# Scores of the first batch from keys in place, and a new order with an engine for each step

## The chip, the cores and the metric

The kernel runs on one core of a Trainium2 chip. Its engines work side by side: TensorE (PE) multiplies matrices, VectorE (DVE) and ScalarE (ACT) work element by element, GpSimd (POOL) does so too but can't read the matrix results in PSUM, and SyncE (SP) issues most of the loads and stores. The metric is the device time of one execution in microseconds; lower is better.

## The reference

Three layers follow one another. The first is attention over 2 batches, 8 heads, 768 positions and 64 columns a head: each query sees the keys less than 16 positions away and, beside them, 24 block summaries (for the keys the maximum of each block of 32, for the values the mean).

```
k_sum = k.reshape(B, H, nb, block, D).max(axis=3)
v_sum = v.reshape(B, H, nb, block, D).mean(axis=3)
scores_l = scale * (q @ k.T), masked to |i - j| < 16
scores_s = scale * (q @ k_sum.T) + log(32)
a = softmax(concat(scores_l, scores_s)); attn = a @ concat(v, v_sum)
h = x @ w_in;  g = max(h, 0) + alpha * min(h, 0);  x = g @ w_out
p = domain_probs / (sum + 1e-9)
out = sum over 4 experts e of p[:, e] * (max(x @ w1[e], 0) @ w2[e])
```

The second layer is a PReLU layer of 512 x 2048 x 512 on 1536 tokens, the third four experts of 512 x 1024 x 512. Everything is float32.

## The kernel before

**Precision.** A float32 factor of the two later layers is split into a high part and the rest, and a product is done as three passes of a faster format. So each activation and weight needs a high part (a copy) and a low part (source minus high part).

**Attention.** A half tile is one batch, 128 queries and four of the eight heads, as two blocks of 64 queries for two pairs of heads: 24 half tiles, numbered 0 to 23, the first twelve in batch 0. Its steps are a chain over the engines. `a_scores` (L199) multiplies the queries with a window tile `kw` of 120 columns, 96 keys around the query block and the 24 block maxima, four products. `a_max` (L207) adds the mask and takes the maximum on VectorE, `a_exp` (L220) is on ScalarE, `a_guard` and `a_recip` (L229, L233) are small VectorE steps, `a_norm` (L236) scales by the reciprocal with four ScalarE instructions, `a_transpose` is on TensorE, `a_copy` (L247) on ScalarE, `a_pv` (L252) multiplies with the values. `a_xh` (ScalarE) and `a_xl` (VectorE) split the result into `xh` and `xl`.

The window tiles come from a copy of the keys that is laid out window by window in memory (`load_kw`, L184, 192 KB a half tile). The block maxima come from the plain keys: `k_load` (L155) brings 384 KB for two heads into a tile `kv`, `k_max` (L158) reduces it on VectorE into `ksum`, and `k_copy` (L161) copies the maxima into both window tiles of a pair of heads. Values go through `v_load`, `v_sum`, `v_rows` and `v_mean` in the same way.

**Weights.** The weights of the PReLU layer arrive as 64-bit numbers and are turned into float32 by integer steps, 32 pieces of 128 x 512: `w_load`, `w_mask` (L294), `w_exp` (ScalarE, L299), `w_mant`, `w_frac` (L311), `w_top`, `w_sign`, `w_value` (L325), `w_high` (ScalarE, L329), `w_low` (L335). All others are on VectorE. `w_mask`, `w_mant` and `w_top` have one tensor as input, the other VectorE steps two.

**PReLU layer, first quarter.** The first four of 16 column groups are done for six blocks of 256 tokens, as soon as a block's half tiles are through. `l1_product` makes 12 passes, four such products a block; `l1_minus`, `l1_prelu`, `l1_high`, `l1_low` follow, then four products `l2a_product` of 12 passes each and their sum into `acc` by `l2a_sum`.

**Order.** All this is written out in `ORDER`, a table of two letters and numbers per step: `sa4` is the scores of half tile 4, `la00` the first product of block 0, `wb5` the mask step of piece 5. Each engine does its steps strictly in the order of the table, and SyncE issues its loads so as well (`wa` weights, `ka`, `va` keys and values for the summaries, `fa` windows, `fb` queries, `fc` value windows). A load waits for its buffer: 3 of queries, 2 of `kv`, 3 of raw weights, 2 of values. The rest of the PReLU layer (512-wide products, from `pa` on) and the experts follow behind the table and are not touched. GpSimd has work only from the experts' first weights on (L366, L373 to L376).

Of the kernel before, what the change touches and what calls it, by code (L numbers as in the profile page):

```python
# [8 lines left out]
F32 = mybir.dt.float32  # L9
# [82 lines left out]
def kernel(  # L92
# [30 lines left out]
    ebias = cst.tile([P, 1], F32, name="ebias")  # L123
    prob_sb = cst.tile([P, NT, NE], F32, name="prob_sb")
# [6 lines left out]

    ident = att1.tile([P, P], F32, name="ident")
    mask = att1.tile([P, 3, NK], F32, name="mask")
    ksum = att1.tile([P, HP, 1, NB], F32, name="ksum")

    kwb = [[att1.tile([P, NK // NB, 2, 2, NB], F32, name=f"kw{hh}{i}") for i in range(2)] for hh in range(2)]
    vs = att1.tile([P, HP, NK], F32, name="vs")
# [8 lines left out]
    def half_tile(i):  # L146
        b, r = divmod(i, 2 * NAC)
        return b, r // 2, r % 2
# [638 lines left out]
```

## Time and profile before

| | |
|---|---|
| three runs | 854.04, 854.30 and 855.51 us, median 854.3 us |
| profiled execution | 854.7 us, of it span 852.9 us |
| TensorE | busy 824.0 us, 97 % of the span |
| VectorE, ScalarE, GpSimd | busy 64 %, 47 % and 39 % |
| loads and stores | 76.61 MB, mean 90 GB/s |

A share over the whole span says little here: the first stretch, with the attention, has other limits than the rest. Times of the views count from the first instruction. A "wait" names what released an engine that stood idle.

### The profile page before, as it was taken

What the parts mean: (1) busy time and instruction counts of PE and PEld (TensorE: products, weight loads), DVE (VectorE), ACT (ScalarE), POOL (GpSimd) and SP (SyncE); (2) the same over time, 40 slices, a digit from 0 to 9 for tenths busy, and PEclk for the clock granted to TensorE, in tenths of its full rate; (3) what the DMA queues carried; (4) which work ended last, traced back from release to release, by engine and by line L of the source; (5) the groups of instructions that cost most, each with busy time, mean ns of one, the idle gap of its engine ahead of it and who ended that gap; (6) DMA issues with size and microseconds to landing.
All of it is one profiled execution on the core that took longest, in us unless ns stands there. A gap on an engine that the chain in (4) does not pass through costs nothing.

```text
span 852.9 us, 12751 instructions
## 1 busy us (share of the span) xinstructions
PE 824.0 (97%) x4622; PEld 734.4 (86%) x4622; DVE 548.9 (64%) x1144; ACT 402.2 (47%) x987; POOL 328.4 (39%) x326
## 2 busy tenths in 40 slices
PE   2799999999999999999999999999999999999998
PEld 2689999888888888989989988888899899898997
DVE  7898566999995446455555567856655555555555
ACT  4999995534443323343343434434534434334340
POOL 0000000000014200376575676775676666756730
PEclk9899999999999999999999999999999999999999
DMA  8998530223221000112213113122322131131201
GB/s 286 290 288 265 155 115 27 98 99 100 86 82 55 26 1 0 50 51 79 71 50 98 51 50 99 50 66 82 125 75 75 50 95 54 50 99 50 75 2 74
DMA packets 39695, 76.61 MB, mean 90 GB/s; under 512 B 3792, under 2 KB 15568, under 8 KB 39632
## 3 DMA queue, kind: packets, MB, share of 16 engines
q1 hardware_dynamic: 39056, 75.51, 27.8%
q8 instruction: 36, 0.59, 0.3%
q10 hardware_dynamic: 576, 0.28, 0.1%
q14 instruction: 27, 0.22, 0.1%
HBM read 72.63 MB, written 3.15 MB: 89 GB/s over the span
## 4 chain that ended last, share of the span: by engine, by line
PE 89%; DVE 6%; DMA 3%; ACT 2%; SPq 0%; issue 0%; ACTq 0%
PE l L413 59%; PE cb L522 15%; PE cd L522 7%; PE ca L522 4%; DMA raw<-in_wa 2%; PE s L205 2%; DVE acc L501 1%; DMA q<-in_qh 1%; PE xps L263 1%; DVE acc L608 1%; PE pt L245 1%; DVE ksum L159 1%; DVE sm L215 0%; DVE xel L483 0%; ACT sm L224 0%
## 5 line engine op out<-in xcount | busy, mean ns | idle before, releaser
L366 POOL TENSOR_TENSOR w0l<-ra,w0h 128x512 fp32r<-128x512 f32 (+1 forms) x64 | 71.1, 1111 | 351.1 <-DVE acc L472 248.3
L608 DVE SCALAR_TENSOR_TENSOR acc<-l,prob_sb,acc 128x512 f32<-128x512 f32 x179 | 133.8, 750 | 74.6 <-PE l L413 74.6
L413 PE MATMUL l<-w1h,gh 128*128 128x512 f32 (+1 forms) x386 | 149.8, 388 | 1.1 <-DVE acc L608 1.1
L413 PE MATMUL l<-w1h,gl 128*128 128x512 f32 (+1 forms) x386 | 150.4, 390 | 0.0
L413 PE MATMUL l<-w1l,gh 128*128 128x512 f32 (+1 forms) x386 | 150.3, 389 | 0.0
L366 POOL TENSOR_TENSOR w0l<-s,w0h 128x512 fp32r<-128x512 f32 x64 | 85.7, 1360 | 5.6 <-ACT w0h L365 5.6
L366 POOL TENSOR_TENSOR w1l<-rb,w1h 128x512 fp32r<-128x512 f32 x64 | 82.0, 1302 | 11.9 <-ACT w1h L365 11.9
L413 PEld LDWEIGHTS l<-w1h,gh 128*128 128x128 f32 x386 | 72.5, 188 | 15.8 <-DVE acc L608 1.6
L413 PEld LDWEIGHTS l<-w1h,gl 128*128 128x128 f32 x386 | 72.4, 188 | 15.0
L413 PE MATMUL l<-xh,w0h 128*128 128x512 f32 (+1 forms) x240 | 84.7, 353 | 0.2 <-ACT ptb L250 0.2
L413 PEld LDWEIGHTS l<-w1l,gh 128*128 128x128 f32 x386 | 72.5, 188 | 14.3
L413 PE MATMUL l<-xl,w0h 128*128 128x512 f32 (+1 forms) x240 | 83.2, 347 | 0.0
L413 PE MATMUL l<-gh,w1h 128*128 128x512 f32 (+1 forms) x240 | 83.1, 350 | 0.0
L413 PE MATMUL l<-xh,w0l 128*128 128x512 f32 (+1 forms) x240 | 83.1, 346 | 0.0
L413 PE MATMUL l<-gh,w1l 128*128 128x512 f32 (+1 forms) x240 | 83.0, 347 | 0.0
L532 ACT ACTIVATE p<-cb 128x384 f32<-128x384 f32 x32 | 15.7, 492 | 140.0 <-PE cb L522 140.0
L413 PE MATMUL l<-gl,w1h 128*128 128x512 f32 (+1 forms) x240 | 80.9, 347 | 0.0
L373 POOL TENSOR_TENSOR s<-ra 128x256 f32<-128x256 f32 x32 | 23.6, 738 | 123.8 <-DMA ra<-in_wb 120.0
L522 PE MATMUL cb<-xeh,w0h 128*128 128x384 f32 x192 | 64.4, 335 | 0.2
L522 PE MATMUL cb<-xeh,w0l 128*128 128x384 f32 x192 | 64.2, 334 | 0.0
L522 PE MATMUL cb<-xel,w0h 128*128 128x384 f32 x192 | 64.2, 334 | 0.0
L539 DVE SCALAR_TENSOR_TENSOR gl<-cb,gh 128x384 fp32r<-128x384 f32 x32 | 17.8, 557 | 55.3 <-ACT gh L538 55.3
(103 smaller groups left out, 1857.2 us busy)
## 6 DMA issues: line engine op xcount, KB each, us to landing
raw<-in_wa SPq DMA_DIRECT2D x32, 512.0 KB, 3.4
ra<-in_wb SPq DMA_DIRECT2D x64, 256.0 KB, 3.1
rb<-in_wb SPq DMA_DIRECT2D x32, 512.0 KB, 3.6
q<-in_qh SPq DMA_DIRECT2D x24, 256.0 KB, 4.9
kw<-in_kw SPq DMA_DIRECT2D x24, 192.0 KB, 5.1
vcat<-in_vw SPq DMA_DIRECT2D x12, 384.0 KB, 5.7
kv<-in_kt SPq DMA_DIRECT2D x8, 384.0 KB, 5.6
kv<-in_vt SPq DMA_DIRECT2D x8, 384.0 KB, 4.7
```

Of the source, the lines that this page charges most:

```text
L159: nc.vector.tensor_reduce(ksum[:, hp, 0], st.pop(("k", b, hp)), axis=AX.X, op=ALU.max)
L205: nc.tensor.matmul(sp[:, u], q[:, u // 2, u % 2], kw[:, :, u // 2, u % 2], start=True, stop=True)
L245: nc.tensor.transpose(pt[0:NK, u], pp[:, u], ident)
L263: nc.tensor.matmul(xps[j * D:(j + 1) * D, u // 2, qb * QB:(qb + 1) * QB], vc[0:NK, qb, h * D:(h + 1) * D], ptb[0:NK, u, j * D:(j + 1) * D] ...
L366: nc.gpsimd.tensor_tensor(lo, src, hi.bitcast(F32), op=ALU.subtract)
L373: nc.gpsimd.tensor_tensor(s12[:, 0], r[:, 0], r[:, 3], op=ALU.add)
L413: ins = nc.tensor.matmul(ps, a, c, start=(i == 0), stop=(i == n - 1))
L501: nc.vector.tensor_tensor(y, p, q, op=ALU.subtract)
L522: nc.tensor.matmul(ps, l, r, start=(first and i == 0), stop=(i == len(terms) - 1), skip_group_check=True)
L532: nc.scalar.activation(v[name], ps, AF.Copy)
L539: nc.vector.scalar_tensor_tensor(gl, src, 0.0, gh.bitcast(F32), op0=ALU.max, op1=ALU.subtract)
L608: nc.vector.scalar_tensor_tensor(acc2[:, t], ps, pe, acc2[:, t], op0=ALU.mult, op1=ALU.add)
```

## The change

Four edits.

The keys of batch 0 are loaded into `kt`, the half of the accumulator `acc1` that belongs to batch 1 and isn't written until the fourth token block's sums. The block maxima are reduced from there, and the scores of batch 0 read keys and maxima in place: one product of 96 columns (two, of 80 and 16, for a block at the start or end of the sequence) and one of 24. `load_kw` and `k_copy` are then used for batch 1 only.

Steps may carry an engine: a trailing `g` in the table puts a normalization (now one instruction of 128 x 480), a `w_value` or a `w_low` on GpSimd, a trailing `v` puts a copy, a ReLU or a normalization on VectorE in place of ScalarE. In the new table 16 normalizations, 13 `w_value` and 11 `w_low` stand on GpSimd, and 39 steps on VectorE that were ScalarE's (9 sums, 8 high parts, 7 `xh`, 6 `l1_minus`, 3 `a_copy`, 3 normalizations, 2 `w_high`, 1 `w_exp`), the first of them behind the second token block's four products.

The table is a new one throughout.

An Exp of a small constant stands at ScalarE's start.

```
 ORDER = (
-    "wa0 ka00 wb0 ka01 wd0 wc0 we0 wa5 fb4 wf0 wg0 kb00 wh0 wa2 fa4 wb5 fa0 fb0 wi0 wc5 wj0 ka02 kb01 "
+    "wa0 wa1 wb0 wd0 we0 ka03 wc0 wd1 wf0 wb1 ka02 wg0 wh0g fb1 ka01 kb03 kb02 sa1 we1 ka00 kb01 wc1 "
...
+    early = cst.tile([P, 1], F32, name="early")
...
-    ksum = att1.tile([P, HP, 1, NB], F32, name="ksum")
+    ksum = att1.tile([P, B, HP, 1, NB], F32, name="ksum")
...
+    def copy(dst, src, on="a"):
+        if on == "v":
+            nc.vector.tensor_copy(dst, src)
+        else:
+            nc.scalar.activation(dst, src, AF.Copy)
...
+    kt = acc1[:, 1]
+
     def k_load(b, hp):
-        st["k", b, hp] = load_kv(kt_in, b, hp)
+        if b == 0:
+            nc.sync.dma_start(out=kt[:, hp], in_=kt_in[b, hp])
+            st["k", b, hp] = kt[:, hp].rearrange("p (n k) -> p n k", k=BLK)
+        else:
+            st["k", b, hp] = load_kv(kt_in, b, hp)
...
     def a_scores(i):
         b, ac, hh = half_tile(i)
-        q, kw = st.pop(("q", i)), st.pop(("kw", i))
+        q = st.pop(("q", i))
+        st["s", i] = sp = ps_s.tile([P, 4, NK], F32, tag="s", name="s")
+        if b == 0:
+            for u in range(4):
+                hp, c0 = 2 * hh + u // 2, (2 * ac + u % 2) * QB - WIN
+                runs = [(0, KW, c0)]
+                if c0 < 0:
+                    runs = [(WIN, KW, 0), (0, WIN, 0)]
+                elif c0 + KW > S:
+                    runs = [(0, KW - WIN, c0), (KW - WIN, KW, S - WIN)]
+                for a, z, c in runs:
+                    nc.tensor.matmul(sp[:, u, a:z], q[:, u // 2, u % 2], kt[:, hp, c:c + z - a], start=True, stop=True)
+                nc.tensor.matmul(sp[:, u, KW:NK], q[:, u // 2, u % 2], ksum[:, b, hp, 0], start=True, stop=True)
+            return
+        kw = st.pop(("kw", i))
...
-    def a_norm(i):
+    def a_norm(i, on="a"):
         pp, r = st["p", i], st.pop(("r", i))
+        if on != "a":
+            eng = nc.vector if on == "v" else nc.gpsimd
+            eng.tensor_tensor(pp, pp, r[:, :, None].to_broadcast([P, 4, NK]), op=ALU.mult)
+            return
...
-    def w_value(p):
+    def w_value(p, on="v"):
         _, e, t = pw[p]
-        nc.vector.tensor_tensor(t, t, e, op=ALU.mult)
-
-    def w_high(p):
+        (nc.gpsimd if on == "g" else nc.vector).tensor_tensor(t, t, e, op=ALU.mult)
+
+    def w_high(p, on="a"):
...
-    def w_low(p):
+    def w_low(p, on="v"):
...
-        nc.vector.tensor_tensor(lo, pw.pop(p)[2], ws[k, i].bitcast(F32), op=ALU.subtract)
+        eng = nc.gpsimd if on == "g" else nc.vector
+        eng.tensor_tensor(lo, pw.pop(p)[2], ws[k, i].bitcast(F32), op=ALU.subtract)
...
     nc.gpsimd.memset(vs, 0.0)
+    nc.scalar.activation(early, ebias, AF.Exp)
...
-            a = x[2:]
-            ins = stage[x[:2]](*((int(a),) if x[0] in "fsntxw" else [int(c) for c in a]))
+            a, on = (x[2:-1], x[-1:]) if x[-1] in "vg" else (x[2:], "")
+            ins = stage[x[:2]](*((int(a),) if x[0] in "fsntxw" else [int(c) for c in a]), *on)
```

On TensorE, the program's first scores before (`s` the scores in PSUM, `kw` a window tile, `q` the queries, `pt` a transpose):

```order
L205 MATMUL s<-kw_96,q 128x120 x4
L205 MATMUL s<-kw_97,q 128x120 x4
L205 MATMUL s<-kw_98,q 128x120 x4
L205 MATMUL s<-kw_99,q 128x120 x4
L245 MATMUL pt<-ident,sm 120x128 x8
```

The same place in the change (`acc` holds the keys, `ksum` the maxima):

```order
L225 MATMUL s<-acc,q 128x80
L225 MATMUL s<-acc,q 128x16
L226 MATMUL s<-ksum,q 128x24
L225 MATMUL s<-acc,q 128x96
L226 MATMUL s<-ksum,q 128x24
```

A query block has two products, or three at an edge, where it had one; half tile 1 is now first, half tile 4 was.

On VectorE, ahead of the first scores before (`ksum` the reduction of keys, `t` and `e` a weight piece's numbers, `w0l` its low part):

```order
L327 TENSOR_TENSOR t<-t,e 128x512
L671 TENSOR_SCALAR prob_s<-prob_s 128x12
L296 TENSOR_SCALAR e<-raw 128x512
L672 RECIPROCAL prob_s<-prob_s 128x12
L673 TENSOR_TENSOR prob_sb<-prob_sb,prob_s 128x48
L338 TENSOR_TENSOR w0l<-t,w0h 128x512
L159 TENSOR_REDUCE ksum<-kv 128x24
L306 TENSOR_SCALAR t<-raw 128x512
L317 TENSOR_SCALAR e<-e 128x512
L296 TENSOR_SCALAR e<-raw 128x512
L163 COPY kw_96<-ksum 128x96
L163 COPY kw_97<-ksum 128x96
```

The same stretch in the change:

```order
L354 SCALAR_TENSOR_TENSOR e<-raw,e 128x512
L172 TENSOR_REDUCE ksum<-acc 128x24
L708 TENSOR_REDUCE prob_s<-prob_sb 128x12
L172 TENSOR_REDUCE ksum<-acc 128x24
L346 SCALAR_TENSOR_TENSOR t<-raw,t 128x512
L709 TENSOR_SCALAR prob_s<-prob_s 128x12
L172 TENSOR_REDUCE ksum<-acc 128x24
L350 TENSOR_SCALAR e<-e 128x512
```

The copies into window tiles are gone, the reductions stand closer together, and the value and low part of the first piece have left VectorE.

On GpSimd, its first tensor work before, which belongs to the experts' weights:

```order
L366 TENSOR_TENSOR w0l<-ra,w0h 128x256
L373 TENSOR_TENSOR s_3602<-ra 128x256
L374 TENSOR_TENSOR s_3602<-s_3602,ra 128x256
L375 TENSOR_TENSOR s_3603<-ra 128x256
L376 TENSOR_TENSOR s_3603<-ra,s_3602 128x256
```

GpSimd's first tensor work in the change (`sm` the probabilities, `r` their reciprocal sums):

```order
L360 TENSOR_TENSOR t<-t,e 128x512
L372 TENSOR_TENSOR w0l<-t,w0h 128x512
L360 TENSOR_TENSOR t<-t,e 128x512
L266 TENSOR_TENSOR sm<-sm,r 128x480 x3
L360 TENSOR_TENSOR t<-t,e 128x512
L266 TENSOR_TENSOR sm<-sm,r 128x480
L372 TENSOR_TENSOR w0l<-t,w0h 128x512
```

Forty such instructions now stand on GpSimd ahead of the experts' first.

## Rows read from the trace of the kernel before

**Rows 1.** Windows: stretch, its us, busy us (instructions) PE, PEld, DVE, ACT, POOL, clock, DMA

```profile
0.00:46.66 46.66, 24.32 (x177) 20.89 (x177) 38.16 (x146) 33.18 (x116) 0.74 (x6) 0.93 0.89 285
46.66:157.03 110.37, 108.51 (x1095) 103.48 (x1094) 81.26 (x300) 92.39 (x327) 0.00 (x0) 1.00 0.53 163
157.03:260.00 102.97, 102.97 (x457) 85.28 (x456) 98.19 (x186) 45.65 (x79) 4.83 (x5) 1.00 0.27 90
```

**Rows 2.** Timeline of TensorE: start, us, operation, [idle before, releaser]

```profile
13.87 3.77 PE L205 MATMUL s<-kw,q 128*128 128x120 f32 x16 [13.87 <-DVE kw L163]
...
45.77 1.12 PE L205 MATMUL s<-kw,q 128*128 128x120 f32 x8 [0.80 <-DMA kw<-in_kw]
46.66 0.36 PE L413 MATMUL l<-xh,w0h 128*128 128x256 f32 x1
...
157.03 0.40 PE L413 MATMUL l<-xh,w0h 128*128 128x512 f32 x1
```

**Rows 3.** Timeline of VectorE ahead of the first product

```profile
5.09 0.43 DVE L296 TENSOR_SCALAR e<-raw 128x512 uint32<-128x512 uint32 x1 [5.09 <-DMA raw<-in_wa]
...
7.65 0.43 DVE L317 TENSOR_SCALAR e<-e 128x512 uint32<-128x512 f32 x1 [1.07 <-ACT e L301]
...
34.99 1.31 DVE L182 TENSOR_SCALAR vcat<-vsps 24x512 f32<-24x512 f32 x2
...
45.55 0.41 DVE L280 TENSOR_TENSOR xl<-xps,xh 128x256 fp32r<-128x256 f32 x1
```

**Rows 4.** Windows: the first 50 us; the last two are DMA share and GB/s

```profile
0.00:50.00 50.00, 27.66 (x225) 24.02 (x226) 41.50 (x161) 36.43 (x128) 0.74 (x6) 0.93 0.90 285
```

**Rows 5.** Chain of waits, VectorE's pitch: start, us, engine, tile, line

```profile
9.84 0.60 DVE t L327
...
11.83 0.86 DVE ksum L159
12.69 0.33 DVE t L306
...
13.70 0.24 DVE kw L163 x2
...
16.28 0.20 DVE sm L215
```

**Rows 6.** The costliest groups: GpSimd's 512-wide low parts, busy us, mean ns

```profile
L366 POOL TENSOR_TENSOR w1l<-rb,w1h 128x512 fp32r<-128x512 f32 x64 | 82.0, 1302 | 11.9 <-ACT w1h L365 11.9
```

**Rows 7.** Timelines of GpSimd and VectorE, 249 to 260 us

```profile
249.61 1.11 POOL L366 TENSOR_TENSOR w0l<-ra,w0h 128x256 fp32r<-128x256 f32 x1 [248.35 <-DVE acc L472]
...
258.14 1.18 POOL L376 TENSOR_TENSOR s<-ra,s 128x256 f32<-128x256 f32 x1
...
250.12 0.88 DVE L317 TENSOR_SCALAR e<-e 128x512 uint32<-128x512 f32 x1
...
253.73 0.67 DVE L327 TENSOR_TENSOR t<-t,e 128x512 f32<-128x512 f32 x1
...
257.93 0.79 DVE L313 SCALAR_TENSOR_TENSOR t<-raw,t 128x512 f32<-128x512 uint32 x1
...
258.76 1.11 DVE L327 TENSOR_TENSOR t<-t,e 128x512 f32<-128x512 f32 x1
```

**Rows 8.** Timelines of GpSimd and VectorE near 507 us, and alone

```profile
506.32 3.60 POOL L366 TENSOR_TENSOR w0l<-s,w0h 128x512 fp32r<-128x512 f32 x2
...
507.77 2.56 DVE L501 TENSOR_TENSOR acc<-acc 128x384 f32<-128x384 f32 x2
...
334.05 0.55 DVE L501 TENSOR_TENSOR acc<-acc 128x384 f32<-128x384 f32 x1
```

**Rows 9.** Chain of waits, TensorE at its full pace

```profile
96.46 0.44 PE pt L245 x4
96.90 0.89 PE s L205 x8
97.78 0.61 PE xps L263 x16
```

More of the change, by code (lines that the diff above doesn't have):

```diff
@@ L153, in load_kv @@
         return t
+    kt = acc1[:, 1]
     def k_load(b, hp):
-        st["k", b, hp] = load_kv(kt_in, b, hp)
+        if b == 0:
[3 more added lines that the diff above has]
+            st["k", b, hp] = load_kv(kt_in, b, hp)
     def k_max(b, hp):
-        nc.vector.tensor_reduce(ksum[:, hp, 0], st.pop(("k", b, hp)), axis=AX.X, op=ALU.max)
+        nc.vector.tensor_reduce(ksum[:, b, hp, 0], st.pop(("k", b, hp)), axis=AX.X, op=ALU.max)
     def k_copy(b, hh):
         for t in kwb[hh]:
-            nc.vector.tensor_copy(t[:, KW // NB], ksum[:, 2 * hh:2 * hh + 2].to_broadcast([P, 2, 2, NB]))
+            nc.vector.tensor_copy(t[:, KW // NB], ksum[:, b, 2 * hh:2 * hh + 2].to_broadcast([P, 2, 2, NB]))
     def v_load(b, hp):
@@ L200, in a_scores @@
         b, ac, hh = half_tile(i)
-        q, kw = st.pop(("q", i)), st.pop(("kw", i))
+        q = st.pop(("q", i))
[13 more added lines that the diff above has]
+        kw = st.pop(("kw", i))
         kw_free[hh].append(kw)
-        st["s", i] = sp = ps_s.tile([P, 4, NK], F32, tag="s", name="s")
         for u in range(4):
@@ L245, in a_transpose, with a_copy @@
             nc.tensor.transpose(pt[0:NK, u], pp[:, u], ident)
-    def a_copy(i):
+    def a_copy(i, on="a"):
         pt = st.pop(("t", i))
         st["b", i] = ptb = att.tile([P, 4, P], F32, tag="ptb", name="ptb")
-        nc.scalar.activation(ptb[0:NK], pt[0:NK], AF.Copy)
+        copy(ptb[0:NK], pt[0:NK], on)
     def a_pv(i):
@@ L273, in x_slice, with a_xh @@
         return slice(None), slice(2 * hh, 2 * hh + 2), slice(t0, t0 + P)
-    def a_xh(i):
-        nc.scalar.activation(xh[x_slice(i)], st["x", i], AF.Copy)
+    def a_xh(i, on="a"):
+        copy(xh[x_slice(i)], st["x", i], on)
     def a_xl(i):
@@ L297, in w_mask, with w_exp @@
         pw[p][1] = e
-    def w_exp(p):
+    def w_exp(p, on="a"):
         e = pw[p][1]
+        if on == "v":
+            nc.vector.tensor_scalar(e, e.bitcast(U32), -EXP_LOW, 0.0, op0=ALU.add, op1=ALU.max)
+            return
         nc.scalar.activation(e, e.bitcast(U32), AF.Relu, bias=ebias)
@@ L323, in w_sign @@
         )
-    def w_value(p):
+    def w_value(p, on="v"):
         _, e, t = pw[p]
-        nc.vector.tensor_tensor(t, t, e, op=ALU.mult)
-    def w_high(p):
+        (nc.gpsimd if on == "g" else nc.vector).tensor_tensor(t, t, e, op=ALU.mult)
+    def w_high(p, on="a"):
         k, i = pieces[p]
         hi = wpool[k].tile([P, DM], F32R, tag="h", name=f"w{k}h")
-        nc.scalar.activation(hi, pw[p][2], AF.Copy)
+        copy(hi, pw[p][2], on)
         ws[k, i] = hi
-    def w_low(p):
+    def w_low(p, on="v"):
         k, i = pieces[p]
         lo = wpool[k].tile([P, DM], F32R, tag="l", name=f"w{k}l")
-        nc.vector.tensor_tensor(lo, pw.pop(p)[2], ws[k, i].bitcast(F32), op=ALU.subtract)
+        eng = nc.gpsimd if on == "g" else nc.vector
+        eng.tensor_tensor(lo, pw.pop(p)[2], ws[k, i].bitcast(F32), op=ALU.subtract)
         ws[k, i] = ws[k, i], lo
@@ L425, in l1_product, with l1_minus @@
         gs[i, c0] = [ps]
-    def l1_minus(i, c0, n):
+    def l1_minus(i, c0, n, on="a"):
         m = gp.tile([P, n], F32, tag="m", name="m", bufs=mbufs)
-        nc.scalar.activation(m, gs[i, c0][0], AF.Relu, scale=-1.0)
+        if on == "v":
+            nc.vector.tensor_scalar(m, gs[i, c0][0], -1.0, 0.0, op0=ALU.mult, op1=ALU.max)
+        else:
+            nc.scalar.activation(m, gs[i, c0][0], AF.Relu, scale=-1.0)
         gs[i, c0].append(m)
@@ L435, in l1_prelu, with l1_high @@
         nc.vector.scalar_tensor_tensor(ps, m, beta[:, i:i + 1], ps, op0=ALU.mult, op1=ALU.add)
-    def l1_high(i, c0, n):
+    def l1_high(i, c0, n, on="a"):
         gh = gp.tile([P, n], F32R, tag="gh", name="gh")
-        nc.scalar.activation(gh, gs[i, c0][0], AF.Copy)
+        copy(gh, gs[i, c0][0], on)
         gs[i, c0].append(gh)
@@ L460, in l2a_product, with l2a_sum @@
         return split3(ps, terms)
-    def l2a_sum(n, d, c0, size):
+    def l2a_sum(n, d, c0, size, on="a"):
         ps = gs.pop(("ps", d, c0))
@@ L469, in l2a_sum @@
             if n == 0:
-                nc.scalar.activation(dst, src, AF.Copy)
+                copy(dst, src, on)
             else:
@@ L641, in block @@
     def block(f):
-        return lambda u, j: f(j, u * C0, C0)
+        return lambda u, j, *on: f(j, u * C0, C0, *on)
     def column(f):
-        return lambda u, d: f(0, d, u * C0, C0)
+        return lambda u, d, *on: f(0, d, u * C0, C0, *on)
     stage = {
```

66 rows, old and new, of the table ORDER are left out of this document.

## Prediction

> **What bounds the kernel now.** I read the windows first, then TensorE's timeline, then the chain of waits and VectorE's timeline for the stretch in which TensorE waits. The windows [rows 1] cut the run where the program changes. Until 46.66 us TensorE is busy for 24.32 us of 46.66; from there to 157.03 us it is busy for 108.51 of 110.37 us, and in the next 103 us without a gap. Those two dates are read in TensorE's timeline [rows 2]: at 46.66 us the first product of the PReLU layer starts, at 157.03 us the first 512-wide product after those of the table. So what the change can win lies ahead of 46.66 us; afterwards TensorE's own work sets the time, and whatever the first product gains the end gains, unless a new wait appears.
>
> Before 46.66 us two things end last. VectorE: the first scores wait 13.87 us for the copies of block maxima into the window tiles [rows 2], and the last low part of x for the first column block starts at 45.55 us [rows 3]. The DMA queues: a load of windowed keys ends a 0.80 us wait just ahead of the first product [rows 2], and over the first 50 us the load rate is 285 GB/s at a busy share of 0.90 [rows 4]. ScalarE, busy for 33.18 of 46.66 us [rows 1], is third, and its work shrinks in the change.
>
> **The change, part by part. VectorE ahead of the first product.** I count VectorE's instructions up to the last low part of x that this product needs, with the pitch that the chain shows [rows 5] and 1.31 us for the pair of mean rows [rows 3]. Before: 9 block reductions at 0.87 (7.8), 8 half tiles of masked maxima at 4 x 0.20 (6.5), the mean rows 1.3, two pairs of copies at 0.24 (0.5), 18 one-input weight steps at 0.34 (6.1), 19 two-input weight steps at 0.60 (11.4), 4 low parts at about 0.33 (1.3): 35.0 us. After: 10 reductions (8.7), 9 half tiles (7.3), 1.3, no copies, 12 one-input steps (4.1), 8 two-input steps (4.8), 4 low parts (1.3): 27.5 us. Seven of the two-input steps have gone to GpSimd; the rest are pieces that the order now makes later. VectorE starts at 5.09 us [rows 3], so before 45.6 + 0.3 - 5.1 - 35.0 = 5.8 us were waits and small work (guards, reciprocals). Of these 1.07 us is the wait for ScalarE's first step, behind its table load [rows 3], which the early Exp takes out of the way; one more guard and reciprocal come in, so I keep 4.9 us. That gives 5.1 + 27.5 + 4.9 = 37.5 us before any price for GpSimd.
>
> **GpSimd beside VectorE.** Up to the first product GpSimd gets 15 instructions that it did not have (4 values, 3 low parts, 8 normalizations), up to the next place where VectorE is late (the first transposes after the block's four products) some 20, each about 1.3 us by its 512-wide rows [rows 6]. They are not free for VectorE. At 249 to 260 us, the one place where the same weight steps run beside GpSimd, VectorE's one-input step of 0.43 us [rows 3] takes 0.88 us, and two two-input steps of 0.67 us take 0.79 and 1.11 us [rows 7]: 1.0 us lost beside five GpSimd instructions (the first and the last of them are shown), 0.2 us each. Near 507 us, where VectorE does little but two-input instructions, two that take 0.55 us alone take 2.56 us, and the two beside them on GpSimd 3.60 us instead of 2.6 [rows 8]: VectorE loses 0.7 us per GpSimd instruction. These are the upper end and the nearer row; the lower end is nothing, where GpSimd runs beside VectorE's waits, and a gain is excluded since VectorE's steps are the same. In the new stretch weight steps and copies are a third of VectorE's time (maxima, reductions and everything from PSUM make up the rest), nearer to the first place, whose share is about half; I take 0.2 us. That is 15 x 0.2 = 3.0 us up to the first product and 1.2 us more up to those transposes.
>
> The Trainium skill, "SBUF — State Buffer", section "Who interferes with whom", says that GpSimd and a VectorE instruction with two SBUF inputs or in a two-port mode share a port pair, that whoever starts first holds it for the whole instruction, and that the other blocks fully. The stretched rows agree in kind; if every one of the 15 blocked VectorE for its full 1.3 us, the first product would come 19.5 us later instead of 3.0, and the kernel would be slower by some 11 us. I don't expect it, since most of VectorE's time in this stretch goes to instructions outside that rule.
>
> **Where the first product then stands.** VectorE: 37.5 + 3.0 = 40.5 us. DMA: in the new queue the last load the products sit behind (queries of half tile 9) ends 10.4 MB; at 285 GB/s that is 36.4 us, and with the 2 us by which such loads come late (the window load that ended the wait at 45.77 us [rows 2] closes the first 12.3 MB, 43.3 us at that rate), the half tile's scores (0.9 us) and a transpose, 40 us. Both agree; with the steps between, 41.2 us instead of 46.66: 5.5 us. Ahead of it TensorE has also done more: one half tile of scores, one of transposes, two of value products, 0.89 + 0.44 + 2 x 0.61 = 2.55 us [rows 9], which leave the later 110.4 us. Against that, VectorE is late once more behind it: by the same count the transposes after the block's four products need 9.5 us more of VectorE than the first product (2 reductions and 2 half tiles 3.4, 7 weight steps 2.9, copies 0.5, small steps 0.5, 6 steps on products and x 2.2), and TensorE's queue between them holds 7.8 us (four products 5.7, one half tile of scores, two of value products), so the difference rises by some 1.6 us, plus the 1.2 us above. Sum: 5.5 + 2.55 - 2.8 = 5.2 us.
>
> **What is hidden.** The scores of the first batch become two products per query block (96 and 24 columns; at the edges three) instead of one of 120. Eight instructions of 120 columns take 0.89 us, 0.111 each [rows 9]. The small ones cost between 0.038 us (the value products' pitch, 0.61/16) and 0.111 us (if the load of the queries sets the pace), the 96-column ones 0.089 to 0.111: 0.13 to 0.89 us per half tile and 0.6 to 1.8 us for the eight edge products, 2 to 12.5 us in all; no gain, since the columns are the same and the instructions more. Eleven of the twelve half tiles lie ahead of the first product, where TensorE idles for 22 us [rows 1]; I take nothing, and the upper end is a rival. The Trainium skill, "TensorE: Matmul & The Clock Gate", section "LDWEIGHTS (loading the stationary operand)", puts a load at its columns divided by 1.2, 107 ns for 128: by that the upper end holds, 12 us instead of nothing on the queue. No row here shows a 24-column product. The twelve window loads that go are 128 x 384 x 4 bytes, 2.4 MB or 8 us of queue at 285 GB/s. This is in the DMA date above. GpSimd's own chain (8 normalizations and 7 steps, 19.5 us, from about 8 us) ends ahead of 40 us even with 0.3 us of blocking on each. In the second half 39 steps move from ScalarE to VectorE at 0.33 to 0.6 us, some 15 us, as much as the 24 weight steps that leave it; VectorE has 29 us free between 46.66 and 157.03 us [rows 1], which covers them. After the table everything is as before.
>
> **The sum.** The profiled execution took 854.7 us (span 852.9); 854.7 - 5.2 = 849.5 us. The median of the three runs is 854.3 us, 0.4 lower, which I leave in the range.
>
> **Rivals.**
> First, slower: GpSimd costs VectorE what it costs near 507 us. For it: normalizations and weight steps come in pairs with VectorE's own weight steps, and VectorE is the bound. Against: the mix. With 0.7 us per instruction instead of 0.2 over 21 instructions, 10.5 us more: 860.0 us. It decides from 0.2 + 5.2/21 = 0.45 us per instruction.
> Second, VectorE is never late and the loads set the date: the values of the fourth query tile arrive with 12.9 MB, at 45.1 us, 47.3 us with the same lateness. TensorE then has about 100 us of table left and 1.1 us of old waits: end of the table at 148.6 us instead of 157.0, 846.3 us; without the lateness 844. For it: 285 GB/s at 0.90; against: VectorE's sum is as late.
> Third, the change gives little: the small products cost 0.111 us each. Then TensorE's queue ahead of the first product holds 17.4 + 11.5 us, plus some 6 us since its first sixteen score instructions took 3.77 us and not 1.8 [rows 2], after a start near 10 us: 45 us, 3.8 us later than forecast, 853.3 us.
>
> **Chances.** A measurement of this kernel can tell 0.2 %, 1.7 us, from no change. Forecast 0.48 (847 to 852.5 us by itself), first rival 0.17, second 0.20, third 0.15. Faster by more than 0.2 %: nearly all of the forecast and the second rival, 0.65; within 0.2 %: the third and the forecast's edge, 0.18; slower 0.17. The range runs from 844.5 us (second rival without lateness) to 857 us (into the first).
>
> **What would show it.** First scores near 10 us instead of 13.9; first product at 39 to 43 us; first 512-wide product at 150 to 153 us with TensorE unbroken behind it; VectorE's weight steps beside GpSimd at 0.2 us a GpSimd instruction over their 0.43 and 0.67; score instructions of 24 columns well under 0.1 us apart. I am wrong if the first product comes after 45 us, if TensorE waits for more than 4 us between it and the end of the table, or if the part after the table changes length.

## The result, and the profile after

The changed kernel takes 857.57 us (median of 19 runs, 854.2 to 869.3), the kernel before 854.88 us beside it (19 runs, 853.4 to 856.2): a ratio of 1.0051, 95 % interval 1.0029 to 1.0073. It is slower by half a per cent, where 849.5 us were forecast, and its runs scatter over 15 us, where those of before scatter over 3. (The ratio leaves out the three slowest executions, 867.9 to 869.3 us, so it isn't that of the two medians; the second execution below, at 869.3 us, shows how such a time comes about.) The profiled execution took 861.5 us (span 859.7), 4 us more than the median.

The windows of the changed kernel, with the columns of [rows 1], cut at the same places: first scores, first product, second group of 512-wide products.

```profile
0.00:10.26 10.26, 0.00 (x0) 0.00 (x1) 3.94 (x9) 2.93 (x4) 1.27 (x7) 1.00 0.82 293
10.26:59.42 49.16, 48.93 (x321) 47.85 (x321) 33.10 (x132) 24.05 (x92) 18.20 (x16) 1.00 0.63 209
59.42:164.26 104.84, 104.26 (x1063) 101.43 (x1061) 94.53 (x321) 67.50 (x236) 28.05 (x23) 1.00 0.47 148
164.26:267.00 102.74, 102.74 (x456) 85.06 (x455) 96.12 (x183) 45.08 (x77) 6.72 (x8) 1.00 0.30 96
```

Ahead of the first product TensorE was busy for 24.32 of 46.66 us before [rows 1]; now it is busy for 48.93 of 49.16 us from its first score on. The product comes at 59.42 us, 12.8 us later. From there to the 512-wide products it takes 104.84 us instead of 110.37, and behind these 695.4 us to the end of the span instead of 695.9: the loss lies wholly ahead of the first product. The waits between 10 and 60 us (who waits for whom, us in total, times, the longest) have turned round: VectorE, and ScalarE behind it, now wait for TensorE.

```profile
ACT sm L250 <- DVE mx L241: 12.5, 6, 4.1
DVE sm L241 <- PE pt L275: 10.4, 4, 5.9
PE s L225 <- DMA q<-in_qh: 10.3, 1, 10.3
...
ACT ptb L151 <- PE pt L275: 6.5, 2, 4.6
DVE sm L241 <- PE s L226: 5.2, 3, 2.1
```

TensorE's timeline answers to [rows 2]:

```profile
10.26 1.04 PE L225 MATMUL s<-acc,q 128*128 128x80 f32 x4 [10.26 <-DMA q<-in_qh]
...
24.43 0.72 PE L225 MATMUL s<-acc,q 128*128 128x96 f32 x2
24.94 0.51 PE L226 MATMUL s<-ksum,q 128*128 128x24 f32 x2
25.28 0.72 PE L225 MATMUL s<-acc,q 128*128 128x96 f32 x2
...
53.52 0.44 PE L225 MATMUL s<-acc,q 128*128 128x96 f32 x2
...
53.96 0.44 PE L225 MATMUL s<-acc,q 128*128 128x96 f32 x2
...
59.42 0.36 PE L447 MATMUL l<-xh,w0h 128*128 128x256 f32 x1
...
164.26 0.40 PE L447 MATMUL l<-xh,w0h 128*128 128x512 f32 x1
```

Starts, not durations, give the pace, since the instructions overlap. Until 52.9 us a query block (96 and 24 columns, two instructions each) takes 25.28 - 24.43 = 0.85 us; from then on 53.96 - 53.52 = 0.44 us. In the kernel before, a block of 120 columns takes 0.22 us at full pace [rows 9]. So two things came together: the split doubles a block's time at full pace, and TensorE stayed at half its pace for 42.7 us, from 10.26 to 52.9. Before, it left the half pace (3.77 us for 16 instructions [rows 2]) at about 25 us. It fell back to it once more, from about 32 to 38.5 us, which the prediction did not use; there 8 instructions take 2.06 us, and the clock column (third from the end of the second line) reads 0.50:

```profile
35.91 2.06 PE L205 MATMUL s<-kw,q 128*128 128x120 f32 x8 [1.15 <-DMA q<-in_qh]
```

```profile
34.00:38.00 4.00, 2.85 (x13) 2.23 (x15) 3.94 (x16) 3.12 (x9) 0.00 (x0) 0.50 1.05 283
```

In the changed kernel the clock column reads 1.00 all the while; that its half pace is the lower of TensorE's two levels (1.2 and 2.4 GHz) all the same is shown by a run below.

### The profile page after: what moved, and what is told of

It is laid out like the page before. It is cut to its first block, busy times and chain, and to the rows that moved or that the text cites. A ratio compares the mean times of both kernels' runs of the same rounds, so it can differ in the third digit from the quotient of the medians.

```text
span 859.7 us, 12920 instructions
## 1 busy us (share of the span) xinstructions
PE 843.8 (98%) x4734; PEld 759.3 (88%) x4734; DVE 557.8 (65%) x1155; ACT 370.5 (43%) x876; POOL 375.9 (44%) x366
## 4 chain that ended last, share of the span: by engine, by line
PE 94%; DVE 4%; DMA 1%; ACT 0%; issue 0%; ACTq 0%; DVEq 0%
PE l L447 59%; PE cb L559 15%; PE cd L559 8%; PE ca L559 4%; PE s L225 3%; PE s L226 2%; PE xps L293 2%; PE pt L275 1%; PE s L231 1%; DMA alpha_sb<-in_alpha 1%; DVE acc L538 1%; DVE acc L645 1%; DVE xel L520 0%; DVE t L346 0%; DVE e L354 0%; DVE sm L241 0%
```

## The experiments

"First product" is the start of the first product of the PReLU layer, "mark" the start of the second group of 512-wide products, as above. Of before they are 46.66 and 157.03 us, of the changed kernel 59.42 and 164.26 us.

**The split alone, in the kernel before.**

```diff
-            nc.tensor.matmul(sp[:, u], q[:, u // 2, u % 2], kw[:, :, u // 2, u % 2], start=True, stop=True)
+            for a, z in [(0, KW // NB), (KW // NB, NK // NB)] if b == 0 else [(0, NK // NB)]:
+                nc.tensor.matmul(
+                    sp[:, u, a * NB:z * NB], q[:, u // 2, u % 2], kw[:, a:z, u // 2, u % 2], start=True, stop=True
+                )
```

> The kernel before with one edit: each score product of the first batch is issued as two, of 96 and of 24 columns, out of the same window tile; loads, copies, engines and order stay. Theory A (the small products and TensorE's low pace under them hold the changed kernel up): in the changed kernel a query block takes 0.85 us at the low pace, against 0.47 us for 120 columns at the low pace here, so 44 blocks ahead of the first product add up to 17 us at the low pace and 10 at the full one to a TensorE that idles 22 us there; part of it shows: first product at 48 to 56 us instead of 46.66, time 856 to 863 us. Rival R (the order, the engines or GpSimd beside VectorE do it): idle time takes the split in, first product within 1 us of 46.66, ratio 0.998 to 1.002.

Measured: 864.05 us (4 runs, 862.3 to 864.7), ratio 1.0112 (1.0096 to 1.0129); first product 56.89, mark 167.05 us. Its timeline of TensorE:

```profile
13.86 7.14 PE L206 MATMUL s<-kw,q 128*128 128x24 f32 x32 [1.16 <-DVE kw L163]
...
53.39 3.65 PE L206 MATMUL s<-kw,q 128*128 128x96 f32 x32
56.89 0.36 PE L416 MATMUL l<-xh,w0h 128*128 128x256 f32 x1
```

32 instructions of both widths take 7.1 us early and 3.65 us from 53.4 us on: the same two paces, with the old order, engines and loads. Theory A holds and asked for a little less; the split by itself costs 9.8 us.

**One product per block, in place.** The product with the maxima is left out.

```diff
-                runs = [(0, KW, c0)]
...
-                for a, z, c in runs:
-                    nc.tensor.matmul(sp[:, u, a:z], q[:, u // 2, u % 2], kt[:, hp, c:c + z - a], start=True, stop=True)
-                nc.tensor.matmul(sp[:, u, KW:NK], q[:, u // 2, u % 2], ksum[:, b, hp, 0], start=True, stop=True)
+                c = min(max(c0, 0), S - NK)
+                nc.tensor.matmul(sp[:, u], q[:, u // 2, u % 2], kt[:, hp, c:c + NK], start=True, stop=True)
```

> The changed kernel with one edit: each query block of the first batch gets one score product of 120 columns of the keys in place, and the product with the block maxima is left out (so the first batch's attention is not the reference's). Order, engines, loads stay. Theory A: TensorE has idle time again, a query block takes 0.47 us at the low pace or 0.22 at the full one, first product at 40 to 46 us instead of 59.4, time 847 to 852 us. Rival R: VectorE beside GpSimd, or the order, keeps the first product late: after 52 us, time 854 to 859 us, with TensorE waiting for VectorE.

Measured: 849.20 us (5 runs, 848.8 to 849.3), ratio 0.9944 (0.9933 to 0.9956); first product 44.77, mark 151.16 us. TensorE's waits up to 160 us, the longest four:

```profile
PE s L220 <- DMA q<-in_qh: 11.9, 2, 11.3
PE s L220 <- DVE mx L235: 2.4, 3, 1.3
PE vsps L187 <- DVE vs L182: 1.6, 1, 1.6
PE pt L269 <- DVE gl L476: 1.1, 1, 1.1
```

VectorE holds TensorE up most again, as the prediction had it: ahead of the first product, without the wait for the first queries, 4.6 of 8.5 us of TensorE's waits are for VectorE. Everything in the change but the split gives 5.0 us; forecast were 5.2.

**Loaded windows in the new order.** Each load fa of the first batch stands behind the fb of its half tile, the copies kc00 and kc01 behind their maxima.

```diff
-    "wa0 wa1 wb0 wd0 we0 ka03 wc0 wd1 wf0 wb1 ka02 wg0 wh0g fb1 ka01 kb03 kb02 sa1 we1 ka00 kb01 wc1 "
...
+    "wa0 wa1 wb0 wd0 we0 ka03 wc0 wd1 wf0 wb1 ka02 wg0 wh0g fb1 fa1 ka01 kb03 kb02 kc01 sa1 we1 ka00 kb01 "
...
```

> The changed kernel's order and engines, with the first batch's keys as they were before: window tiles loaded for each half tile (behind the load of its queries), the copies of the block maxima into them, one score product of 120 columns. Theory A: as the run with one product in place, but with 2.4 MB more to load (8 us of queue at 285 GB/s) and four more copies on VectorE: first product at 43 to 50 us, time 848 to 855 us. Rival R: after 52 us, 855 to 860 us.

Measured: 853.22 us (12 runs, 849.9 to 855.7), ratio 0.9988 (0.9975 to 1.0001); first product 48.69, mark 154.02 us. Theory A: without the split the new order is not slower than before, but 12 more loads and four copies cost 4.0 us against the run in place.

**Zeros ahead of the scores.**

```diff
+        zero, warm = vs.rearrange("p a b -> p (a b)"), ps_s.tile([P, 4, NK], F32, tag="s", name="warm")
+        for _ in range(6):
+            nc.tensor.matmul(warm.rearrange("p a b -> p (a b)"), zero[:, 0:P], zero, start=True, stop=True)
```

> The changed kernel with six products of zeros (128 x 480, float32) issued on TensorE ahead of the first scores, in the 10.26 us in which it waits for the first queries; all else stays. Theory A1 (the low pace is what TensorE starts with and leaves only when it has been kept busy with wide work): the first scores run at 0.45 us per query block instead of 0.85, the queue ahead of the first product shrinks from 49 to some 25 us, VectorE is the bound again, first product at 40 to 46 us, 847 to 852 us, and the scatter from run to run goes. Theory A2 (under the small products the pace falls to the low level whatever went before): the first few blocks at 0.45 us, then 0.85 again, first product after 54 us, time 854 to 860 us. Rival R: pace up but first product still after 52 us, with TensorE waiting for VectorE.

Measured: 857.02 us (12 runs, 854.9 to 870.7), ratio 1.0048 (1.0018 to 1.0078); first product 51.04, mark 157.89 us. Its window from 20 to 30 us (columns as above) and TensorE's timeline:

```profile
20.00:30.00 10.00, 10.00 (x49) 10.00 (x49) 5.58 (x28) 5.36 (x24) 2.72 (x3) 0.50 0.67 211
```

```profile
1.32 7.66 PE L702 MATMUL warm<-vs 128*128 128x480 f32 x12 [1.32 <-POOL vs L674]
10.31 0.62 PE L225 MATMUL s<-acc,q 128*128 128x80 f32 x4 [1.33 <-DMA q<-in_qh]
12.04 0.40 PE L226 MATMUL s<-ksum,q 128*128 128x24 f32 x2 [1.11 <-DVE ksum L172]
...
24.93 0.72 PE L225 MATMUL s<-acc,q 128*128 128x96 f32 x2
25.44 0.51 PE L226 MATMUL s<-ksum,q 128*128 128x24 f32 x2
...
33.96 0.44 PE L225 MATMUL s<-acc,q 128*128 128x96 f32 x2
```

The first scores run at the full pace; after two waits of 1.33 and 1.11 us and a few small products it falls at 13.5 us and comes back at 33.8. Here the record has the clock at 0.50 where a block takes 0.85 us: the half pace is 1.2 GHz, and in the changed kernel's profile the record missed it. A2 is right that the pace falls under these products, and wrong on how long it stays; a start at full pace does not help the median. The profiled execution is one of the faster ones, at 855.97 us.

**Without GpSimd.** The run with one product, with each g struck from the table.

```diff
-    "wa0 wa1 wb0 wd0 we0 ka03 wc0 wd1 wf0 wb1 ka02 wg0 wh0g fb1 ka01 kb03 kb02 sa1 we1 ka00 kb01 wc1 "
...
+    "wa0 wa1 wb0 wd0 we0 ka03 wc0 wd1 wf0 wb1 ka02 wg0 wh0 fb1 ka01 kb03 kb02 sa1 we1 ka00 kb01 wc1 "
...
```

> The run with one score product of 120 columns in place (849.2 us, first PReLU product at 44.77 us; the block maxima's product is left out here too), with one more edit: the steps that the table gives to GpSimd stand at their old engines (normalizations on ScalarE, values and low parts on VectorE). Theory P1 (GpSimd costs VectorE 0.2 us per instruction, and takes more off it than that): VectorE gets 7 two-input steps of 0.6 us back ahead of the first product and loses 3 us of stretching, first product 0 to 3 us later, time 849 to 852 us. Theory P2, the first rival of the prediction (0.7 us per instruction): without GpSimd the first product comes 4 us or more earlier, time 843 to 846 us.

Measured: 859.97 us (5 runs, 859.5 to 860.6), ratio 1.0074 (1.0060 to 1.0087); first product 49.21, mark 161.86 us. Both theories missed: leaving GpSimd out costs 10.8 us. ScalarE is what ends last without it (waits, as above):

```profile
PE pt L268 <- ACT sm L262: 5.2, 4, 1.9
PE pt L268 <- DVE gl L475: 2.5, 2, 2.2
```

Part of the price is TensorE's pace. The mark comes 10.7 us later; of these 3.4 us are added idle time of TensorE, and 7.3 us are longer busy time on the same instructions (136.0 against 128.7 us up to the mark). After the longer waits TensorE is back at half pace near 42 and 63 us (clock 0.57 from 40.7 to 44.6 us, 0.50 from 62 to 64). What the move to GpSimd is worth at one and the same pace is not shown.

What GpSimd costs VectorE is read from the groups of VectorE from 10 to 60 us (count | busy us, mean ns), with GpSimd and then without:

```profile
L251 DVE TENSOR_SCALAR r<-sume 128x4 f32<-128x4 f32 x12 | 5.3, 448 | 0.0
L348 DVE SCALAR_TENSOR_TENSOR e<-raw,e 128x512 uint32<-128x512 uint32 x6 | 4.1, 682 | 0.0
...
L320 DVE TENSOR_SCALAR e<-raw 128x512 uint32<-128x512 uint32 x5 | 3.5, 704 | 0.0
```

```profile
L347 DVE SCALAR_TENSOR_TENSOR e<-raw,e 128x512 uint32<-128x512 uint32 x5 | 3.4, 687 | 0.0
...
L250 DVE TENSOR_SCALAR r<-sume 128x4 f32<-128x4 f32 x11 | 1.7, 162 | 0.1
...
L319 DVE TENSOR_SCALAR e<-raw 128x512 uint32<-128x512 uint32 x4 | 1.7, 421 | 0.0
```

One-input steps (the 14 of their three kinds go from 0.42 to 0.66 us), guards (0.16 to 0.45), copies of maxima (0.20 to 0.40) and one small step on `prob_s`, the experts' shares (0.17 to 1.27), are stretched by 3.3 + 3.4 + 0.8 + 1.1 = 8.6 us beside 22 instructions of GpSimd: 0.39 us each. Two-input steps are not (0.682 and 0.687).

**A wide product ahead of each half tile's scores.**

```diff
         if b == 0:
+            nc.tensor.matmul(
+                sp.rearrange("p a b -> p (a b)"), q[:, 0, 0], q.rearrange("p a b c -> p (a b c)")[:, 0:4 * NK],
+                start=True, stop=True,
+            )
             for u in range(4):
```

> The changed kernel with one product more ahead of each half tile of the first batch's scores: float32, 480 columns, the queries against themselves, into the sums that the scores then overwrite. By the run with zeros ahead of the scores such a product takes 0.64 us on the mean of a stretch at both paces, so this adds 12 x 0.64 = 7.7 us of work or more to a TensorE that was never idle after 10.26 us. Theory A1 (what holds TensorE at the low pace is a queue of nothing but small products): the pace goes to 0.45 us per query block before 25 us, as where one product has 120 columns, the queue shrinks from 49 to some 36 us, first product at 45 to 50 us, time 849 to 855 us, less scatter. Theory A2 (the pace is a matter of chance or of what lies outside the scores): pace low until 40 us or more, the added work in full, first product after 62 us, time 862 us or more.

Measured: 864.14 us (4 runs, 862.8 to 864.3), ratio 1.0117 (1.0103 to 1.0131); first product 60.24, mark 166.32 us. Neither theory whole: the half pace ends at 34.9 us, 18 us sooner, but a wide product takes 1.73 us at it and 0.81 at the full one, and the added work eats the gain. (The 0.64 us of the expectation were one of a product's two instructions.) A2 has the time, though not its first product, and A1 part of the cause.

**Keys copied into the windows by ScalarE.** The table is that of the run with loaded windows, and the scores read window tiles, one product of 120 columns.

```diff
         st["kw", i] = t = kw_free[hh].pop(0)
+        if b == 0:
+            for qb in range(2):
+                c0 = (2 * ac + qb) * QB - WIN
+                runs = [(0, KW, c0)]
...
+                for a, z, c in runs:
+                    n = min(NB, z - a)
+                    dst = t[:, a // NB:(z + NB - 1) // NB, :, qb, a % NB:a % NB + n].rearrange("p a h n -> p h a n")
+                    src = kt[:, 2 * hh:2 * hh + 2, c:c + z - a].rearrange("p h (a n) -> p h a n", n=n)
+                    nc.scalar.activation(dst, src, AF.Copy)
+            return
```

> The changed kernel with its keys of the first batch in place loaded once, but copied by ScalarE into the window tiles of the kernel before (two copies of 128 x 192 per half tile, six at the edges), so that a query block has one score product of 120 columns; the copies of the maxima return too. No load is added. Theory A: first product at 44 to 48 us as with one product in place, plus 8 us of copies on a ScalarE that is half idle; time 848 to 852 us, less than the run with loaded windows and than the kernel before. Rival S: the copies stand in ScalarE's queue ahead of the exponentials and make them late; first product after 50 us, 854 us or more.

Measured: 850.19 us (5 runs, 849.2 to 851.3), ratio 0.9958 (0.9946 to 0.9971); first product 45.28, mark 151.97 us. TensorE's scores wait for the copies for 2.0 us. It is at the full pace near 20 us, falls back (clock 0.50 from 24 to 26 us) and keeps the full pace from about 26 us on:

```profile
PE s L233 <- ACT kw L212: 2.0, 2, 1.5
```

Theory A. This computes the reference in full and is faster than both kernels, than the one before by 0.4 %.

**The changed kernel twice more.**

> The changed kernel as it is, once more, for a second profiled execution, since its times lie between 854.2 and 869.3 us. If the length of TensorE's low pace sets the time (in the first profile it ended at 52.5 us, the first product came at 59.4 us and the run took 861.5 us): each us by which it ends earlier brings the first product 0.5 us earlier, down to some 46 us where VectorE is the bound, and the time with it. If the scatter lies elsewhere: the same 52 us with another time, or another length after 266 us.

> The changed kernel a third time, with the same expectations as the second: 0.5 us of first product for each us of low pace, and the time with it, or the scatter elsewhere.

Measured: 869.34 us, first product 64.60, mark 171.24 us; and 862.68 us, 59.79, 164.62 us. In the first of them TensorE's half pace lasts beyond the scores, into the first products (256 columns, 0.21 us apart, then 0.12):

```profile
64.60 0.56 PE L447 MATMUL l<-xh,w0h 128*128 128x256 f32 x1
64.96 0.41 PE L447 MATMUL l<-xl,w0h 128*128 128x256 f32 x1
65.17 0.41 PE L447 MATMUL l<-xh,w0l 128*128 128x256 f32 x1
...
68.55 0.28 PE L447 MATMUL l<-xh,w0h 128*128 128x256 f32 x1
68.67 0.28 PE L447 MATMUL l<-xl,w0h 128*128 128x256 f32 x1
```

In three executions the half pace ended at 52.9, 53.3 and 68.4 us, and they took 861.5, 862.7 and 869.3 us: the time follows. (No execution at 854 to 858 us, where 11 of the 19 lie, was traced; that the half pace ends earlier there is an inference.) The first of the three gives TensorE's work ahead of the first product, at full pace: 49.16 - 0.23 (a wait) - 42.5 / 2 = 27.7 us. Start, this work, half of the half-paced time (without waits) and the waits then give the others within 1.2 us:

| run | start | busy at half pace, us | added or waited | sum | measured |
|---|---|---|---|---|---|
| third execution | 10.3 | 42.5 | 0.5 | 59.8 | 59.79 |
| second execution | 10.6 | all, 54.0 | | 65.3 | 64.60 |
| zeros ahead | 10.3 | 19.4 | 2.2 | 49.9 | 51.04 |
| wide products | 10.6 | 24.3 | 11 x 0.81 | 59.4 | 60.24 |

**The single product issued twice.** The product with the maxima is left out here too.

```diff
-                nc.tensor.matmul(sp[:, u], q[:, u // 2, u % 2], kt[:, hp, c:c + NK], start=True, stop=True)
+                for _ in range(2):
+                    nc.tensor.matmul(sp[:, u], q[:, u // 2, u % 2], kt[:, hp, c:c + NK], start=True, stop=True)
```

> The run with one score product of 120 columns in place (the block maxima's product left out), with each of these products issued twice into the same sums. A query block then has as many products and loads of queries as in the changed kernel, but 240 columns instead of 120. Theory W (narrow products hold TensorE at its low pace): it leaves the low pace near 25 us as with one product, a block takes 0.44 us from then on, first product at 45 to 48 us, time 849 to 852 us, little scatter. Theory N (the number of products and loads in an unbroken queue holds it): a block takes 0.94 us until 40 us or later, first product after 56 us, time 858 us or more, with scatter.

Measured: 848.65 us (4 runs, 848.3 to 849.0), ratio 0.9931 (0.9914 to 0.9947); first product 45.05, mark 150.46 us.

```profile
10.89 10.78 PE L221 MATMUL s<-acc,q 128*128 128x120 f32 x64 [10.89 <-DMA q<-in_qh]
...
22.53 1.94 PE L221 MATMUL s<-acc,q 128*128 128x120 f32 x16
```

Theory W: as many products and loads of queries as in the changed kernel and twice the columns, and it costs nothing; 16 instructions take 1.94 us from 22.5 us on. Neither the count of products nor their loads hold the half pace here. What differs from the changed kernel is the 24-column product, and with it the columns per block, 240 instead of 120.

**The maxima's product widened, to 96 and to 120 columns.** Zeros stand ahead of the maxima; the product goes first and the keys overwrite 96 columns. The edit with 96 (with 120: NK for KW, and sp[:, u] whole):

```diff
+    kwide = att1.tile([P, HP, KW], F32, name="kwide")
...
-        nc.vector.tensor_reduce(ksum[:, b, hp, 0], st.pop(("k", b, hp)), axis=AX.X, op=ALU.max)
+        dst = kwide[:, hp, KW - NB:] if b == 0 else ksum[:, b, hp, 0]
+        nc.vector.tensor_reduce(dst, st.pop(("k", b, hp)), axis=AX.X, op=ALU.max)
...
+                nc.tensor.matmul(sp[:, u, NK - KW:], q[:, u // 2, u % 2], kwide[:, hp], start=True, stop=True)
                 for a, z, c in runs:
...
-                nc.tensor.matmul(sp[:, u, KW:NK], q[:, u // 2, u % 2], ksum[:, b, hp, 0], start=True, stop=True)
...
+    nc.gpsimd.memset(kwide, 0.0)
```

> The changed kernel, its keys read in place, with one edit: the product with the block maxima is widened from 24 to 96 columns (72 columns of zeros ahead of the maxima) and issued first, into columns 24 to 120 of the sums; the product with the keys then overwrites the first 96. Nothing is left out. Edge blocks keep their 80 and 16 columns. Theory W (narrow products hold TensorE at its low pace): a query block has 192 columns instead of 120, yet the pace rises near 25 us, first product at 45 to 48 us, time 849 to 852 us, faster than the kernel before, little scatter. Theory N (the number of products does): no change against the changed kernel, 856 us or more, with scatter.

> As the run with the maxima's product of 96 columns (852.2 us median, its runs either near 850.5 or near 854), but with 120 columns: 96 of zeros, 24 of maxima, issued first over the whole 120 columns of the sums; the keys overwrite 96. Theory W: more columns per product bring TensorE to its full pace as early in every run, 849.5 to 851.5 us, with less scatter, and still no cost at the full pace (0.45 us per block). If the narrow 16-column products of the edges or something else decide: the same two groups of times, median 852.

Measured with 96: 852.16 us (12 runs, 850.0 to 855.8), ratio 0.9980 (0.9963 to 0.9997), first product 46.18, mark 152.25 us. With 120: 850.76 us (11 runs, 849.7 to 854.3; nine of them at 851.0 or less), ratio 0.9966 (0.9953 to 0.9979), 46.84 and 152.99 us. The timeline with 120:

```profile
16.36 0.67 PE L226 MATMUL s<-kwide,q 128*128 128x120 f32 x2
16.83 0.59 PE L228 MATMUL s<-acc,q 128*128 128x96 f32 x2
17.21 0.67 PE L226 MATMUL s<-kwide,q 128*128 128x120 f32 x2
...
22.66 0.41 PE L226 MATMUL s<-kwide,q 128*128 128x120 f32 x2
22.91 0.37 PE L228 MATMUL s<-acc,q 128*128 128x96 f32 x2
23.11 0.41 PE L226 MATMUL s<-kwide,q 128*128 128x120 f32 x2
```

A block takes 0.85 us at half pace and 0.45 at full, as with 24 columns: the 96 columns of zeros are free, and TensorE leaves the half pace at 20 us instead of 53. Theory W; the scatter shrinks and does not go. Widening a product also raises the columns per block, so these runs do not tell which of the two counts. Both compute the reference in full, and the one with 120 columns is faster than both kernels (than the one before by 0.3 %) with the keys still read in place.

## Why the prediction was wrong

**The step that failed** is "What is hidden": the split was costed at nothing, since TensorE idles for 22 us ahead of the first product. At the full pace that would have held: 10.26 + 27.7 = 38 us, well ahead of the 44.8 us at which VectorE lets the first product come in the run with one product. The half pace was the mistake. The step left it out, and the third rival carried [rows 2]'s half pace over as some 6 us at the start of TensorE's work; under the split scores it lasted 43 to 58 us in the three traced executions. A block cost 0.22 us more than with 120 columns at the full pace, 0.40 more at half (0.85 against 0.45, the 16 instructions from 19.81 to 23.37 us before the change), and TensorE's queue became the bound: 8.4 us of time against the run with one product (857.57 and 849.20 us), 9.8 us in the kernel before.

**The third rival had the mechanism and a term too small.** Its TensorE queue of 17.4 + 11.5 = 28.9 us at full pace measured 27.7. Its 6 us for the half pace measured 21.2 (half of 42.5) in the first traced execution, so there the first product came at 59.4 us, not 45, and the end was slower, not the same.

**What held.** First scores at 10.26 us; TensorE without gaps behind the first product (0.6 us of waits up to the mark); the part behind the mark unchanged; and without the split the time, 849.2 us for 849.5. That the sum came out right is in part luck, with two errors of nearly the same size: the first product came at 44.8 us, 3.6 later than forecast, and the stretch to the mark was 4.0 us shorter than before [rows 1], where I had it 0.25 us longer, since I let VectorE be late once more there.

**GpSimd.** 0.39 us per instruction, between the 0.2 that I took and the 0.45 from which the first rival decides. With 15 instructions that is an estimated 2.9 us of the 3.6 by which the first product was late without the split. So that rival was not it; but I weighed only the price: the same instructions on ScalarE and VectorE cost 10.8 us, TensorE's pace included. The Trainium skill, "SBUF — State Buffer", section "Who interferes with whom", names two-input instructions of VectorE and those in two-port modes as what shares a port pair with GpSimd. The traces agree on one-input steps, 0.42 to 0.66 us, if these are in such a mode, which no row shows; the two-input steps show no stretch (0.687 and 0.682 us), though whether they start later is not seen in a duration.

**The price of a small product.** Bounds of 0.038 and 0.111 us were given per instruction of 24 columns, and the upper one held. The queries' loads into TensorE (one per instruction; L226 is the 24-column product) start 0.11 us apart at the full pace and 0.21 at half:

```profile
24.79 0.55 PEld L226 LDWEIGHTS s<-ksum,q 128*128 128x128 f32 x2
25.21 0.55 PEld L225 LDWEIGHTS s<-acc,q 128*128 128x128 f32 x2
...
54.16 0.30 PEld L226 LDWEIGHTS s<-ksum,q 128*128 128x128 f32 x2
54.38 0.30 PEld L225 LDWEIGHTS s<-acc,q 128*128 128x128 f32 x2
```

A block of two products takes the same 0.85 and 0.45 us with 24, 96 or 120 columns in the second, so here its columns cost nothing beside the load. The Trainium skill, "TensorE: Matmul & The Clock Gate", section "LDWEIGHTS (loading the stationary operand)", puts the load of 128 columns at 107 ns. The trace agrees at the full pace, 0.11 us, and shows twice that at half. So the queue did grow by some 10 us at full pace (44 blocks at 0.22 us), near the upper end of the prediction, and was hidden only at the full pace.

**Signs.** "24-column instructions well under 0.1 us apart" and "first product after 45 us" were the right ones to look at: the first failed at 0.11 us at the full pace and 0.21 at half, the second at 59.4.

What stays open: why the half pace ends when it does. In one and the same kernel it ended at 52.9, 53.3 and 68.4 us, with zeros ahead of the scores at 33.8, with wide products between them at 34.9; that narrow products prolong it is shown by widening them, the rule behind it is not, nor whether the width of a product or the columns per block counts.

## What to carry to other kernels

Work put into an engine's idle time is hidden only at the pace that the engine has there: price it at the lowest pace that the trace shows for that stretch, and ask whether the new instructions change the pace. Where narrow products are added to TensorE's queue in a stretch at half pace, try padding or joining them; columns of zeros cost nothing here. And read the pace from the distance of like instructions, not from the clock's column.

## What was not expected of the hardware

- TensorE can be busy for 10.00 of 10 us and stay at half its pace for over 40 us: 42.7 us in the changed kernel, 57.8 in its second execution (10.6 to 68.4), with 24-column products in the queue; with 96 or 120 columns in their place 8 us (11.6 to 19.3, and 12.0 to 20).
- The granted clock read 1.00 through such a stretch in one kernel and 0.50 in another, at the same 0.85 us per block.
- A product of 120 columns issued a second time cost nothing: 848.65 against 849.20 us.
- Beside GpSimd, VectorE's guard on 128 x 4 elements took 0.45 instead of 0.16 us.
